# A gated MLP on one Trainium2 core: three steps of the gate change engines

## Chip, cores, metric

The kernel runs on one core of one Trainium2 chip, in one launch. The metric is the device time of an execution in microseconds (us); lower is better.

## What is computed

Three parts follow each other: an attention in which a query sees only the keys of its own cluster, a mixing by Fourier transforms with a plain MLP, and a gated MLP with a convolution of width 3 along the sequence. Batch 2, sequence 768, model width 512. The change touches the last part alone:

```python
def _moe2_ref(x, w_in, conv_w, w_out) -> np.ndarray:   # x (2, 768, 512), d_ff 1024
    h = np.maximum(x @ w_in, 0.0)
    ...
    for k in range(K):                                  # K = 3
        conv_out += conv_w[k][None, None, :] * hp[:, k:k + S, :]
    gate = 1.0 / (1.0 + np.exp(-conv_out))
    return (h * gate @ w_out).astype(np.float32)
```

`hp` is `h` with a zero row before and behind.

## The kernel before, in words

The engines are TensorE (PE; matmuls, with PEld for its weight loads), VectorE (DVE, `V` in the code), ScalarE (ACT, `A`), GpSimd (POOL, `G`) and SyncE (SP), which issues the DMAs here.

Products are made in near fp32 precision from pairs of numbers: a value is split into a high part, its cast to fp32r, and a low part, the value less the high one. `pass3` (lines 77 to 80) adds three matmuls for each product: high times high (L78), and the two mixed ones (L79, L80).

The gated MLP (from line 901 on) works in 16 blocks: two batches `b`, and in each eight blocks `f` of 128 hidden features. The features lie on the partitions, the 768 positions of the sequence in a row's elements. Each block has two halves.

- `mlp2_up(b, f)`, lines 797 to 815. `split_w` casts the block's weights to their high part on ScalarE (L778, `whb`) and makes the low part on POOL (L780, `wlb`). TensorE makes `u` in two halves of 384 positions, 12 matmuls each, in one of two PSUM banks by turns; ScalarE's relu (L806) empties each bank into `h2`. `h2` has a column of zero on either side (the memsets L801, L802). Then the gate: VectorE makes the convolution in three steps, a product (L808) and two products with a sum (L809, L810), in the tile `cv`; ScalarE makes the sigmoid in place (L811), POOL multiplies by `h2` (L812), VectorE casts to the high part `gH` (L814) and subtracts for the low part `gL` (L815).
- `down(1, b, f, side)`, lines 817 to 836. For each of six tiles of 128 positions three matmuls add to that tile's own PSUM bank `acc`. After the last block of a batch, VectorE and ScalarE by turns copy the six banks to `y`, one of three buffers (L833, L835), from where SyncE sends them out (L836).

The loop on lines 905 to 908 calls `mlp2_up` two blocks ahead of `down`. `cv`, `h2`, `gH` and `gL` have two buffers each, the split weights four. In the first six calls of `down`, `side` is `gate_in(1)` (lines 838 to 855): after the third tile TensorE transposes one tile of the second batch's input into one of the two banks of `u`, ScalarE casts it (L853), and VectorE subtracts for the low part (L854). The order on each engine is fixed when the program is built, by the scheduler of the tile framework; each engine works through its own queue in order, and an instruction that waits holds up all behind it.

Of the kernel before, what the change touches and what calls it, by code (L numbers as in the profile page):

```python
# [15 lines left out]
AF = mybir.ActivationFunctionType  # L16
ALU = mybir.AluOpType
# [3 lines left out]
B, H, S, D = 2, 8, 768, 64  # L21
# [21 lines left out]
def tile_net(ctx, tc, qk, v, cen, w12, w34, conv, dft, odd, out):  # L43
    nc = tc.nc
    V, A, G, T = nc.vector, nc.scalar, nc.gpsimd, nc.tensor

    def f32(ap):
        return ap.bitcast(F32)
# [186 lines left out]
    def norm(b, bank, lp):  # L235

        X = U[:, 6 * b:6 * b + 6, :]
        stats, ys, os = {}, {}, {}

        def stat(t):  # L240
            if b not in uns:
                uns[b] = up_[b].tile([128, 2, 4, S], F32R, tag="un", bufs=1, name=f"un{b}")
            st = lp.tile([128, 6], F32, tag="st", bufs=2, name=f"st{b}{t}")
            V.bn_stats(st, X[:, t])
            mv = lp.tile([128, 2], F32, tag="mv", bufs=3, name=f"mv{b}{t}")
            V.bn_aggr(mv, st)
            rs = lp.tile([128, 1], F32, tag="rs", bufs=3, name=f"rs{b}{t}")
            V.tensor_scalar(rs, mv[:, 1:2], 1e-6, None, ALU.add)
            stats[t] = (mv, rs)

        def root(t):
            rs = stats[t][1]
            G.tensor_tensor(rs, rs, half[:, 2:3], ALU.pow)

        def scale(t):
            mv, rs = stats[t]
            y = ys[t] = lp.tile([128, DM], F32, tag="y", bufs=1, name=f"y{b}{t}")
            V.tensor_scalar(y, X[:, t], mv[:, 0:1], rs, ALU.subtract, ALU.mult)

        def swap(t):  # L260
            o = os[t] = bank(f"unT{b}{t}").rearrange("p (c n) -> p c n", c=4)
            for c in range(4):
                T.transpose(o[:, c], ys[t][:, 128 * c:128 * c + 128], ident)
            A.copy(uns[b][:, 0, :, 128 * t:128 * t + 128], o)

        def low(t):
            tk = slice(128 * t, 128 * t + 128)
            V.tensor_sub(uns[b][:, 1, :, tk], os[t], f32(uns[b][:, 0, :, tk]))

        return stat, root, scale, swap, low  # L270
# [30 lines left out]
    def up_half(o, w, x, i):  # L301
        tk = slice(384 * i, 384 * i + 384)
        for c in range(4):
            sl = slice(128 * c, 128 * c + 128)
            pass3(o, w[0][:, sl], w[1][:, sl], x[:, 0, c, tk], x[:, 1, c, tk], c == 0, c == 3)
# [4 lines left out]
    with ExitStack() as actx:  # L310
# [7 lines left out]
        def slot(name):  # L318
            turn[0] = (turn[0] + 1) % 3
            return ps.tile([128, 2, 512], F32, tag=f"s{turn[0]}", bufs=1, name=name)  # L320
# [37 lines left out]
        t = slot("warm_up")  # L358
# [27 lines left out]
        for i in range(2):  # L386
            t = ap.tile([128, NT, 2, 130], F16, name=f"V16_{i}")
# [273 lines left out]
        stat, root, scale, swap, low = norm(0, lambda name: slot(name)[:, 0], dp)  # L661
# [111 lines left out]
    def up_bank(name):  # L773
        return bank("up", 2, name)

    def split_w(p, bufs, k, f, name, eng=G):
        wh = p.tile([128, 1024], F32R, tag="wh", bufs=bufs, name=f"wh{name}")
        A.copy(wh, w32[k, f])  # L778
        wl = p.tile([128, 1024], F32R, tag="wl", bufs=bufs, name=f"wl{name}")
        eng.tensor_sub(wl, w32[k, f], f32(wh))  # L780
        return wh[:, 0:512], wl[:, 0:512], wh[:, 512:1024], wl[:, 512:1024]
# [15 lines left out]
    def mlp2_up(b, f):  # L797
        gp = gps[0]
        w = ws[1, b, f] = split_w(gp, 4, "b", f, f"b{b}_{f}")
        h2 = gp.tile([128, S + 2], F32, tag="h2", bufs=2, name=f"h2{b}{f}")  # L800
        V.memset(h2[:, 0:1], 0.0)  # L801
        V.memset(h2[:, S + 1:S + 2], 0.0)  # L802
        for i in range(2):
            o = up_bank(f"u{b}{f}{i}")[:, 0:384]
            up_half(o, w, xs[b], i)
            A.activation(h2[:, 1 + 384 * i:385 + 384 * i], o, AF.Relu)  # L806
        t = gp.tile([128, S], F32, tag="cv", bufs=2, name=f"cv{b}{f}")
        V.tensor_scalar(t, h2[:, 0:S], cw[:, 3 * f:3 * f + 1], None, ALU.mult)  # L808
        V.scalar_tensor_tensor(t, h2[:, 1:S + 1], cw[:, 3 * f + 1:3 * f + 2], t, ALU.mult, ALU.add)  # L809
        V.scalar_tensor_tensor(t, h2[:, 2:S + 2], cw[:, 3 * f + 2:3 * f + 3], t, ALU.mult, ALU.add)  # L810
        A.activation(t, t, AF.Sigmoid)  # L811
        G.tensor_mul(t, t, h2[:, 1:S + 1])  # L812
        g = hs[1, b, f] = [gp.tile([128, S], F32R, tag=n, bufs=2, name=f"{n}{b}{f}") for n in ("gH", "gL")]
        V.tensor_copy(g[0], t)  # L814
        V.tensor_sub(g[1], t, f32(g[0]))  # L815

    def down(s, g, f, side, when=(2,)):
# [60 lines left out]
    cw = wp.tile([128, 24], F32, tag="cw", bufs=1, name="cw")  # L878
# [22 lines left out]
    gps.append(pool(ctx, "gp", side="right"))  # L901
    side = gate_in(1)
    mlp2_up(0, 0)
    mlp2_up(0, 1)
    for n in range(8 * B):
        if n + 2 < 8 * B:
            mlp2_up((n + 2) // 8, (n + 2) % 8)
        down(1, n // 8, n % 8, side)
# [72 lines left out]
```

## Time and profile before

| | |
|---|---|
| median of 3 runs | 752.48 us (lowest 751.13; one of the three took 2342.31) |
| the profiled execution | 750.55 us |
| its span (first to last instruction) | 748.8 us |
| TensorE busy | 698.7 us, 93% |
| VectorE busy | 536.4 us, 72% |
| ScalarE busy | 345.9 us, 46% |
| POOL busy | 271.2 us, 36% |
| granted clock of TensorE, mean | 0.979 |
| the gated MLP | from about 595 us to the end |

All times of the trace are counted from the start of the span. A row of the timeline gives the start, the duration, the engine, the line, the operation, its output and inputs, their shapes, how often it occurs in the row, and in square brackets how long the engine stood idle just before it and what ended that wait. Matmuls follow each other in a pipeline, so the duration of one is longer than the step from one to the next. The releaser is the event that came last, and need not be the one that had been missing longest.

### The profile page before, as it was taken

To read this page: it belongs to the slowest core of one execution; us is meant where nothing else is said; L and a number is where in the kernel's file an instruction comes from. 1 tells how busy PE (TensorE), PEld (TensorE's weight loads), DVE (VectorE), ACT (ScalarE), POOL (GpSimd) and SP (SyncE) were. 2 spreads that over 40 slices of the span, in tenths; PEclk is the share of its full clock that TensorE was granted. 3 is DMA by queue.
4 is the path that set the end of the run, shared out by engine and by line. 5 is a ranking of instruction groups with operands and counts; after the bars stand their busy time and mean duration, and the time that the engine had idled before them with its cause. 6 is when DMAs were issued, how large, how long until landed. Compare 5 with 4: busy or idle time off the path is not lost.

```text
span 748.8 us, 12517 instructions
## 1 busy us (share of the span) xinstructions
PE 698.7 (93%) x5090; PEld 623.2 (83%) x5090; DVE 536.4 (72%) x754; ACT 345.9 (46%) x492; POOL 271.2 (36%) x189
## 2 busy tenths in 40 slices
PE   8898999897998996989999999999999999999996
PEld 6787788786897885878988899999999788898984
DVE  7778989679977998999379937765111268777664
ACT  3576868586466685334234433433222233333321
POOL 8154644455244544131041003222232154443441
PEclk9999999999799999899999999999999999999999
DMA  7637678462533431214104321430000000002002
GB/s 219 173 78 209 184 196 251 107 196 59 157 71 79 92 116 59 98 71 169 57 0 169 116 109 57 168 113 1 1 0 1 1 0 1 1 1 84 1 1 84
DMA packets 19937, 66.47 MB, mean 89 GB/s; under 512 B 2868, under 2 KB 5928, under 8 KB 16808
## 3 DMA queue, kind: packets, MB, share of 16 engines
q1 hardware_dynamic: 19448, 61.93, 28.5%
q0 software_dynamic: 432, 3.75, 1.5%
q8 instruction: 40, 0.66, 0.3%
q14 instruction: 17, 0.14, 0.1%
HBM read 40.94 MB, written 5.77 MB: 62 GB/s over the span
## 4 chain that ended last, share of the span: by engine, by line
PE 48%; DVE 34%; ACT 5%; DMA 4%; POOL 4%; issue 3%; SPq 1%; POOLq 0%; DVEq 0%
PE up L78 5%; DVE m L533 5%; PE up L80 5%; PE up L79 5%; PE acc L80 5%; PE acc L78 5%; PE acc L79 5%; DVE gH L814 5%; DMA vraw<-v 3%; POOL cv L812 3%; PE av L590 3%; PE t L562 2%; DVE cv L809 2%; PE s L528 2%; DVE cv L810 2%
## 5 line engine op out<-in xcount | busy, mean ns | idle before, releaser
L578 POOL TENSOR_TENSOR p<-p,p 128x768 f16<-128x768 f32 x61 | 109.7, 1802 | 115.4 <-ACT p L573 81.7
L566 ACT ACTIVATE p<-t,cbias 128x768 f32<-128x768 f32 x96 | 86.2, 898 | 54.1 <-PE t L564 44.3
L533 DVE TENSOR_REDUCE m<-s 128x1 f32<-128x768 f32 x96 | 90.1, 943 | 13.1 <-PE s L530 6.7
L80 PE MATMUL up<-un,wla 128*128 128x384 f32 x248 | 83.9, 339 | 1.6 <-DVE wla L780 1.6
L78 PE MATMUL up<-un,wha 128*128 128x384 f32 x248 | 84.1, 339 | 0.7 <-DVE YsL L178 0.5
L780 POOL TENSOR_TENSOR wla<-wa,wha 128x1024 fp32r<-128x1024 f32 x16 | 38.5, 2404 | 126.6 <-ACT wha L778 126.6
L79 PE MATMUL up<-un,wha 128*128 128x384 f32 x248 | 83.9, 338 | 0.0
L795 DVE SCALAR_TENSOR_TENSOR hL<-up,hH 128x384 fp32r<-128x384 f32 x62 | 34.2, 552 | 65.6 <-ACT hH L794 65.4
L590 PEld LDWEIGHTS <-p 128*128 128x128 f16 x1728 | 61.1, 100 | 21.6 <-issue 15.4
L590 PE MATMUL av<-V,p 128*128 128x65 f16 x1728 | 73.2, 197 | 5.4 <-POOL p L578 3.6
L573 ACT CAST p<-p 128x768 f16<-128x768 f32 x91 | 75.5, 830 | 1.5
L78 PE MATMUL acc<-wha,hH 128*128 128x512 f32 x186 | 73.7, 396 | 0.0
L80 PE MATMUL acc<-wha,hL 128*128 128x512 f32 x186 | 72.7, 391 | 0.0
L79 PE MATMUL acc<-wla,hH 128*128 128x512 f32 x186 | 72.5, 390 | 0.0
L562 PE MATMUL t<-X 128*128 128x384 f32 x192 | 55.6, 371 | 16.8 <-DVE m L533 14.2
L794 ACT ACTIVATE hH<-up 128x384 fp32r<-128x384 f32 x62 | 30.4, 490 | 75.0 <-PE up L80 74.9
L528 PE MATMUL s<-X 128*128 128x384 f32 x192 | 57.0, 379 | 5.9 <-DVE m L533 4.7
L814 DVE CAST gH<-cv 128x768 fp32r<-128x768 f32 x16 | 35.3, 2209 | 31.3 <-POOL cv L812 31.3
L778 ACT CAST wha<-wa 128x1024 fp32r<-128x1024 f32 x31 | 32.5, 1048 | 52.2 <-PE acc L80 46.3
L812 POOL TENSOR_TENSOR cv<-cv,h 128x768 f32<-128x768 f32 x16 | 25.4, 1590 | 78.1 <-ACT cv L811 78.1
L562 PEld LDWEIGHTS t<-X 128*128 128x128 f32 x192 | 31.9, 193 | 25.1 <-DVE m L533 15.8
L530 PE MATMUL s<-Y 96*128 96x384 f32 x192 | 50.6, 345 | 1.2 <-DMA Y<-G 1.2
(311 smaller groups left out, 1652.0 us busy)
## 6 DMA issues: line engine op xcount, KB each, us to landing
rawa<-w SPq DMA_DIRECT2D x14, 1024.0 KB
rawb<-w SPq DMA_DIRECT2D x8, 1024.0 KB
raw<-qk SPq DMA_DIRECT2D x7, 768.0 KB
X<-G SPq DMA_DIRECT2D x14, 384.0 KB
Y<-G SPq DMA_DIRECT2D x14, 384.0 KB
DC<-dft POOLq DMA_DIRECT2D x2, 1671.0 KB, 7.1
vraw<-v SPq DMA_DIRECT2D x8, 384.0 KB
out<-y SPq DMA_DIRECT2D x12, 256.0 KB
```

Of the source, the lines that this page charges most:

```text
L78: T.matmul(o, sH, mH, start=start, stop=False)
L79: T.matmul(o, sH, mL, start=False, stop=False)
L80: T.matmul(o, sL, mH, start=False, stop=stop)
L528: T.matmul(t[:, c, 0:384], X[:, 0, sl], X[:, 1, 384 * c:384 * c + 384], start=True, stop=False)
L530: T.matmul(t[:, c, 0:384], Y[0:96, 0, sl], Y[0:96, 1, 384 * c:384 * c + 384], start=False, stop=True)
L533: V.tensor_reduce(m6s[h][:, i:i + 1], t[:, :, 0:384], AX.XY, ALU.max, negate=True)
L562: T.matmul(t[:, c, 0:384], X[:, 1, sl], X[:, 0, 384 * c:384 * c + 384], start=True, stop=False)
L566: A.activation(p.rearrange("p (c n) -> p c n", c=2), t[:, :, 0:384], AF.Exp, bias=cbias, scale=0.125)
L573: A.copy(p16[:, 0], p32s[n])
L578: eng.tensor_sub(p16[:, 1], p, p16[:, 0])
L590: T.matmul(o, p16[:, k, 128 * j:128 * j + 128], v16[:, i, h % 2, 65 * part:65 * part + 65], start=(i + j + k + part == 0), stop=(i == 5), ...
L814: V.tensor_copy(g[0], t)
```

## The change

Three lines of `mlp2_up` change engines, and no value that they compute. The convolution's first product goes from VectorE to ScalarE, as an activation Copy with the weight as its scale. The product of the gate and `h2` goes from POOL to VectorE. The cast to `gH` goes from VectorE to ScalarE.

```diff
@@ def mlp2_up(b, f)
         t = gp.tile([128, S], F32, tag="cv", bufs=2, name=f"cv{b}{f}")
-        V.tensor_scalar(t, h2[:, 0:S], cw[:, 3 * f:3 * f + 1], None, ALU.mult)
+        A.activation(t, h2[:, 0:S], AF.Copy, scale=cw[:, 3 * f:3 * f + 1])
         V.scalar_tensor_tensor(t, h2[:, 1:S + 1], cw[:, 3 * f + 1:3 * f + 2], t, ALU.mult, ALU.add)
         V.scalar_tensor_tensor(t, h2[:, 2:S + 2], cw[:, 3 * f + 2:3 * f + 3], t, ALU.mult, ALU.add)
         A.activation(t, t, AF.Sigmoid)
-        G.tensor_mul(t, t, h2[:, 1:S + 1])
+        V.tensor_mul(t, t, h2[:, 1:S + 1])
         g = hs[1, b, f] = [gp.tile([128, S], F32R, tag=n, bufs=2, name=f"{n}{b}{f}") for n in ("gH", "gL")]
-        V.tensor_copy(g[0], t)
+        A.copy(g[0], t)
         V.tensor_sub(g[1], t, f32(g[0]))
```

The scheduler orders the queues anew. On VectorE, in a block of the second batch (`cv_7473` is this block's convolution, `h_7442` its `h2`, `gH_7479` and `gL_7480` its parts; `h_7568` is the `h2` of a later block):

```order
-L808 TENSOR_SCALAR cv_7473<-h_7442,cw 128x768
 L809 SCALAR_TENSOR_TENSOR cv_7473<-h_7442,cw,cv_7473 128x768
 L810 SCALAR_TENSOR_TENSOR cv_7473<-h_7442,cw,cv_7473 128x768
-L814 CAST gH_7479<-cv_7473 128x768
+L812 TENSOR_TENSOR cv_7473<-cv_7473,h_7442 128x768
 L801 MEMSET h_7568 128x1
 L802 MEMSET h_7568 128x1
 L815 TENSOR_TENSOR gL_7480<-cv_7473,gH_7479 128x768
```

The product stands where the cast stood, and the first product of the convolution is gone from the queue.

On ScalarE, in the same block (`whb_5_7564` is the high part of the weights two blocks on; the two relus that follow belong to the next block, `h_7505`):

```order
 L806 ACTIVATE h_7442<-u_7445 128x384
 L806 ACTIVATE h_7442<-u_7459 128x384
+L808 ACTIVATE cv_7473<-h_7442,cw 128x768
 L811 ACTIVATE cv_7473<-cv_7473 128x768
 L778 CAST whb_5_7564<-wb_6216 128x1024
+L814 CAST gH_7479<-cv_7473 128x768
 L806 ACTIVATE h_7505<-u_7508 128x384
 L806 ACTIVATE h_7505<-u_7522 128x384
+L808 ACTIVATE cv_7536<-h_7505,cw 128x768
```

The cast to `gH` stands between the weight cast and the next block's relus.

On ScalarE in the opening (`h_6710`, `h_6755` and `h_6800` are the `h2` of blocks 0, 1 and 2, `gH_6747` is the high part of block 0):

```order
 L806 ACTIVATE h_6710<-u_6713 128x384
 L806 ACTIVATE h_6710<-u_6727 128x384
+L808 ACTIVATE cv_6741<-h_6710,cw 128x768
 L806 ACTIVATE h_6755<-u_6758 128x384
 L811 ACT_TABLE_LOAD
 L811 ACTIVATE cv_6741<-cv_6741 128x768
 L806 ACTIVATE h_6755<-u_6772 128x384
+L808 ACTIVATE cv_6786<-h_6755,cw 128x768
+L814 CAST gH_6747<-cv_6741 128x768
 L806 ACTIVATE h_6800<-u_6803 128x384
 L806 ACTIVATE h_6800<-u_6817 128x384
+L808 ACTIVATE cv_6831<-h_6800,cw 128x768
```

Block 1's first product and block 0's cast now stand in front of block 2's relus. On TensorE the one difference is in the first `acc`: its first L80 stands behind the L78 and L79 of the second tile too.

## Rows read from the trace of the kernel before

**Rows 1.** The page, section 4: the chain that ended last, by engine.
```profile
PE 48%; DVE 34%; ACT 5%; DMA 4%; POOL 4%; issue 3%; SPq 1%; POOLq 0%; DVEq 0%
PE up L78 5%; DVE m L533 5%; PE up L80 5%; PE up L79 5%; PE acc L80 5%; PE acc L78 5%; PE acc L79 5%; DVE gH L814 5%; DMA vraw<-v 3%; POOL cv L812 3%; PE av L590 3%; PE t L562 2%; DVE cv L809 2%; PE s L528 2%; DVE cv L810 2%
```
**Rows 2.** Busy time by stage: window, its length, each engine, PEclk, DMA share, GB/s.
```profile
690.00:735.00 45.00, 45.00 (x223) 40.27 (x222) 30.84 (x35) 12.20 (x20) 17.27 (x9) 1.00 0.01 5
```
**Rows 3.** Timeline of VectorE: one block, and the last block's L809.
```profile
698.56 1.02 DVE L809 SCALAR_TENSOR_TENSOR cv<-h,cw,cv 128x768 f32<-128x768 f32 x1
...
703.23 2.77 DVE L814 CAST gH<-cv 128x768 fp32r<-128x768 f32 x1 [2.60 <-POOL cv L812]
...
706.10 0.96 DVE L815 TENSOR_TENSOR gL<-cv,gH 128x768 fp32r<-128x768 f32 x1
...
707.63 1.02 DVE L809 SCALAR_TENSOR_TENSOR cv<-h,cw,cv 128x768 f32<-128x768 f32 x1
...
732.63 1.02 DVE L809 SCALAR_TENSOR_TENSOR cv<-h,cw,cv 128x768 f32<-128x768 f32 x1
```
**Rows 4.** Timelines of ScalarE and of POOL in the same block.
```profile
700.66 0.85 ACT L811 ACTIVATE cv<-cv 128x768 f32<-128x768 f32 x1 [5.96 <-DVE cv L810]
701.41 1.03 ACT L778 CAST whb<-wb 128x1024 fp32r<-128x1024 f32 x1
702.35 0.87 ACT L806 ACTIVATE h<-u 128x384 f32<-128x384 f32 x2
...
701.65 1.55 POOL L812 TENSOR_TENSOR cv<-cv,h 128x768 f32<-128x768 f32 x1 [5.14 <-ACT cv L811]
703.16 2.42 POOL L780 TENSOR_TENSOR wlb<-wb,whb 128x1024 fp32r<-128x1024 f32 x1
```
**Rows 5.** Timeline of TensorE: first matmuls of `u`, of `acc`, and of the next `u`.
```profile
698.21 0.34 PE L78 MATMUL u<-x,whb 128*128 128x384 f32 x1
...
702.45 0.40 PE L78 MATMUL acc<-whb,gH 128*128 128x512 f32 x1
...
706.65 0.34 PE L78 MATMUL u<-x,whb 128*128 128x384 f32 x1
```
**Rows 6.** Timeline of TensorE from 606 us on: the rows with a wait.
```profile
608.39 0.44 PE L78 MATMUL u<-x,whb 128*128 128x384 f32 x1 [0.41 <-ACT h L806]
...
612.38 0.50 PE L80 MATMUL acc<-whb,gL 128*128 128x512 f32 x1 [1.06 <-DVE gL L815]
619.51 0.44 PE L78 MATMUL u<-x,whb 128*128 128x384 f32 x1 [0.59 <-DVE h L802]
...
647.40 0.42 PE L78 MATMUL u<-x,whb 128*128 128x384 f32 x1 [1.01 <-DVE x L854]
...
688.98 0.50 PE L78 MATMUL acc<-whb,gH 128*128 128x512 f32 x1 [1.11 <-DVE y L833]
...
737.91 0.50 PE L78 MATMUL acc<-whb,gH 128*128 128x512 f32 x1 [1.58 <-DVE gH L814]
738.98 0.50 PE L80 MATMUL acc<-whb,gL 128*128 128x512 f32 x1 [0.33 <-DVE gL L815]
```
**Rows 7.** Timelines of POOL and VectorE: the opening, and a `gH` late in the stage.
```profile
595.41 9.80 POOL L780 TENSOR_TENSOR wlb<-wb,whb 128x1024 fp32r<-128x1024 f32 x4 [17.01 <-PE acc L79]
...
602.97 3.06 DVE L809 SCALAR_TENSOR_TENSOR cv<-h,cw,cv 128x768 f32<-128x768 f32 x1
...
730.44 0.56 DVE L814 CAST gH<-cv 128x768 fp32r<-128x768 f32 x1 [2.60 <-POOL cv L812]
```
**Rows 8.** Busy time by stage, as rows 2: one microsecond of the last `acc`.
```profile
740.00:741.00 1.00, 1.00 (x4) 0.72 (x4) 0.20 (x1) 0.10 (x1) 0.00 (x0) 0.50 0.07 20
```
**Rows 9.** Timeline of the end: first output copy, last matmul, last output copy.
```profile
739.52 0.58 ACT L835 COPY y<-acc 128x512 f32<-128x512 f32 x1 [3.94 <-PE acc L80]
...
744.13 0.39 PE L80 MATMUL acc<-whb,gL 128*128 128x512 f32 x1
...
744.82 0.69 DVE L833 COPY y<-acc 128x512 f32<-128x512 f32 x1 [0.92 <-DMA out<-y]
```
**Rows 10.** The chain that ended last, in order of time: start, length, what.
```profile
742.69 2.01 DMA out<-y
```

## Prediction

> **What bounds the kernel now.** I read the chain of waits first. In the whole span it is TensorE for about half and VectorE for a third, and among its costliest steps stand VectorE's cast L814 (gH) [rows 1]. All lines of the change lie in the second MLP, so I went to that stretch. The table by stage shows a puzzle: from 690 to 735 us TensorE is busy in all of the time at full clock [rows 2], and still VectorE could matter. To see why, I laid one feature block f (16 of them: two batches of eight) beside itself on each engine.
>
> VectorE's block takes from the start of one L809 to the next 9.07 us (698.56 to 707.63) [rows 3]. Every step of it hands on: L809 and L810 2.10 together, then the sigmoid on ScalarE (0.99 until POOL starts), POOL's product L812 (1.58 until gH starts), gH 2.87 until gL starts, then gL and the next block's L808, 1.53 [rows 3, 4]. The sum is 9.07, so this is a closed ring with no slack. TensorE's block is 24 `u` matmuls in 4.24 us and 18 `acc` matmuls in 4.20, together 8.44 [rows 5]. The ring is thus 0.63 us a block slower than TensorE. TensorE doesn't show it at once, since `up` runs two blocks ahead of `down`; it eats up the lead, and waits at the end.
>
> So I listed every place where TensorE waits behind a line of the change [rows 6]. The bracket is the idle time; as matmuls overlap (0.34 us long at a step of 0.177, 0.39 at 0.233), the loss from start to start is the bracket plus 0.16. That gives 0.57 (608.39, ScalarE's relu held up behind a sigmoid), 1.22 (612.38, gL), 0.75 (619.51, the memset row is only the last event; the relu stood behind the sigmoid and the weight cast), 1.17 (647.40, an x transpose's bank not yet read by VectorE), 1.27 (688.98, an accumulator of the first batch not yet copied by VectorE, which was at gH and gL), 1.74 and 0.49 (737.91 and 738.98, gH and gL of the last block). Together 7.2 us. Behind the last two the granted clock is 0.50, that is 1.2 GHz, in the row of 740 to 741 [rows 8]; TensorE had been idle for 1.58 and 0.33 us just before it fell [rows 6]. From 738.98 to the last matmul at 744.13 there are 15 steps, which at 0.233 are 3.5 us and took 5.15: another 1.65 [rows 6, 9]. All that the change can win is about 8.9 us, 1.2% of the time.
>
> **The change part by part.** Per block VectorE loses L808 and gH and gets the product; POOL loses the product and keeps only the weight split L780; ScalarE gets L808 and gH.
>
> *The product on VectorE.* The nearest row is gL, which also reads two fp32 tiles: 0.96 us; the dearest is L809 at 1.02 [rows 3]. I take 0.96, against POOL's 1.55 [rows 4].
>
> *L808 and gH on ScalarE.* Not seen there before. The nearest row is the sigmoid on the same 128x768, 0.85; above lies the cast of 128x1024 at 1.03, below half of the pair of relus on 128x384, 0.43 [rows 4]. I take 0.85 each. gH thus gets dearer than its free price on VectorE, 0.56 (730.44) [rows 7], but cheaper than the 2.77 that it costs beside L780.
>
> *Who holds whom.* gH took 2.77 where POOL's L780 (2.42) had started 0.07 us earlier, and 0.56 where POOL had nothing left to do [rows 3, 4, 7]. L809 at 602.97 took 3.06 while four L780 filled POOL from 595.41 on, and 1.02 later [rows 3, 7]. So VectorE's work on two SBUF tiles and POOL's shut each other out. The Trainium skill says so in "SBUF — State Buffer", section "Who interferes with whom": a VectorE instruction with two SBUF inputs and a GpSimd one that reads SBUF can't run together, and the one that comes second waits for the whole of the first. The trace agrees (3.06 against 1.02). By that rule the new product is as exposed as gH was, and gL too.
>
> Which of them meets L780? L780 needs the weight cast L778, which ScalarE issues after the sigmoid and which starts 0.75 after it; with its 1.03 and 0.14 to the start on POOL (as from sigmoid to product, [rows 4]) L780 begins 1.9 us after the sigmoid's start. The product can start 0.95 after it and is through at 1.9, so it comes first. gL, after gH on ScalarE, would start at 2.85 and comes second. gH ended 0.42 after L780 did (706.00 against 705.58), so I expect gL at 5.2, a record of some 2.3 us in place of 0.96. This costs nothing: it lies beside matmuls, as the next sum shows. It would cost if gL were wanted within 9 us of `u`.
>
> *The new chain against TensorE.* Let T be the end of a block's `u` (the start of the next `acc`, 702.45 in the block shown). The relu pair ends at T+0.77 [rows 4, 5]. Then L808 to 1.66, L809 and L810 to 3.77, sigmoid 3.80 to 4.65, product 4.75 to 5.71, gH to 6.60, gL to 7.6, or to 9.0 if held. `acc` of this block starts only after two more blocks' worth of matmuls, at T+16.9. So in the steady blocks nothing waits. In the last block no `u` lies between: `acc` 13 and 14 take 8.40, then gH is wanted at T+8.4 and gL 0.47 later. Nothing is left on POOL by then, so they are there 1.8 and 1.3 us early. The last waits (1.74 and 0.49) go, and the clock has no pause behind which to fall (1.65).
>
> *New orders on ScalarE.* gH of block f waits for the product and stands in front of the relus of f+1. As a ring: relus 0.87, L808 0.89, L809 and L810 2.10, sigmoid 0.95, product 1.01, gH 0.89, in all 6.7 us a block. This is under TensorE's 8.44, so the bank of `u` is read in time. The x copies (L853, L854) and the output copies lie beside L809 and the sigmoid on whichever of the two engines is free then.
>
> *The opening.* L809 of block 0 still can't run before POOL's fourth L780 is through (602.97 to 606.03 now [rows 7]). L808 no longer delays that L780, so I take 0.3 off, and the 0.57 at 608.39 shrinks to 0.27. By the steps above its product is then through at 608.7; ScalarE does L808 of block 1 first and gH to 609.6, VectorE L809 of block 1 first and gL to 610.8. TensorE starts `acc` at 610.3 and wants gL at 611.2, since its first L80 now stands behind four matmuls where it stood behind two. The 1.22 goes. Relu 3 is no longer behind sigmoid 2 at its late hour: 0.75 goes. 1.17 and 1.27 go because the copies that TensorE waits for there no longer stand on VectorE behind a held gH.
>
> *The end.* From the last `acc`'s start to the last output copy it takes 6.91 us now (737.91 to 744.82) [rows 6, 9]. At full clock a tile takes 0.70. The copy of tile 5 needs tile 2's buffer (three of them), so its landing: 1.87 us to tile 2's last matmul, 0.54 to the copy (from the last matmul of a tile at 738.98 to 739.52), 0.58 the copy, 2.01 the transfer, 0.15 the issue: 5.15 [rows 6, 9, 10]. The transfer now hides part of the clock's 1.65. Gain 1.76.
>
> **Sum.** 0.3 + 1.22 + 0.75 + 1.17 + 1.27 + 1.74 + 1.76 = 8.2 us. The profiled execution took 750.55 (span 748.8 and 1.75 around it), the median of the runs shown is 752.48 and the lowest 751.13. From 751.5 in their midst the forecast is 743.3. Bounds: 8.9 less what the end hides is the most that waits can give back; the least, with ScalarE's two at 1.03 and all waits of the opening kept, is about 4.8.
>
> **Rivals.**
> *A, the opening keeps its waits* (0.20). In the first blocks ScalarE gets L808 and gH in front of relus that TensorE waits for, with a margin of only 0.4 us at gL; and the x copy at 647 comes to stand behind the product. For it: two of the early waits already run through ScalarE. Against: the product leaves POOL and its late start. The gains up to 647 (3.4) stay away: 8.2 less 3.4 is 4.8, time 746.7.
> *B, slower: the ring through ScalarE decides* (0.05). Its place is gH in front of the next relus, its price whatever lengthens the ring beyond 6.7. The second half of block 3's `u` begins now at 619.51, so this `u` ends at 621.6; less the 2.3 won by then it is 619.4, and L809 follows 1.7 later at 621.1. L809 of block 15 stands at 732.63 [rows 3]. With eleven rings and a last one of 6.7 (no weights are left to split) it comes later than that from a ring of 9.5 on. If the product were held for one L780 it would end 2.9 later, 0.42 behind POOL; the ring is then 9.6, and L809 of block 15 0.8 late, a tie. At 9.9 it is 736.7, some 4 us late, time 755.5. Against it: the product's lead of 0.95 us on L780. By the lock rule of the Trainium skill, above, the product is held if POOL gets there first.
> *C, more than the waits* (0.07): with the product gone from POOL the matmuls step faster, say by 1% of 16 blocks of 8.44, 135 us: another 1.4, and with the rest of the opening's 0.57 some 1.7, time 741.6. No row speaks for it.
> *D, the clock falls at the end all the same* (0.08): 1.5 of the 1.76 stays, time 744.8.
>
> **How the numbers follow.** The forecast has 0.60. It, C and D lie between 741 and 745; A lies at 746.7, B around and beyond 751. With the spread of the runs shown (1.4 us) on either side, and up to the foot of B, I take 740.5 to 750.5. A measurement of this kernel can tell about 2%, 15 us, from no change. No case with a place in the trace wins 15 us, and B needs a ring of 10.9 to lose them: faster 0.02, within 0.96, slower 0.02.
>
> **What would show it.** gL and no longer gH held by L780 (some 2.3 us beside 0.96), the product at 0.96, L808 and gH on ScalarE at 0.85, the L809 step at TensorE's 8.44, no wait of TensorE on gH or gL in the last block, and the clock at 1.00 behind 730. Wrong would be: a product of over 2 us, relus that start late behind gH with TensorE idle on `u`, or a last block that waits again.

## The result and the profile after

The changed kernel takes 742.39 us (median of 4 runs, 740.63 to 745.13) against 751.81 for the kernel before (4 runs beside it). The ratio of the fast runs is 0.9891, with a 95% interval of 0.9848 to 0.9934; one run before took 2342.31 us, which lifts that median and stands outside the ratio. The change makes the kernel about 1% faster, inside the 2% that counts as no change. The forecast was 743.3. The profiled execution took 740.75 with a span of 739.0; before it was 750.55 and 748.8.

The start of the second MLP shifts by up to 6 us from trace to trace, behind work whose lines the change doesn't touch. So I compare what I call the stage: from the first `u` matmul to the end of the span. Before it lasts 153.46 us (595.34 to 748.8), after 144.82 (594.18 to 739.0). The gain is 8.64, the forecast's sum 8.2. The other 1.16 of the 9.8 us between the spans lies ahead of the stage.

The chain that ended last, by engine and by line (the page of the kernel after, section 4):

```profile
PE 66%; DVE 21%; DMA 5%; ACT 3%; issue 3%; POOL 1%; SPq 1%; DVEq 0%; POOLq 0%; ACTq 0%
PE acc L78 8%; PE acc L79 8%; PE acc L80 8%; PE up L78 5%; PE up L80 5%; PE up L79 5%; DVE m L533 5%; DMA vraw<-v 4%; PE av L590 3%; PE u L80 3%; PE u L78 3%; PE u L79 3%; PE s L528 3%; PE t L562 3%; PE t L564 2%
```

TensorE has risen from 48% to 66% and VectorE has fallen from 34% to 21% [rows 1]. gH, the product and the two sums, four of the costliest steps of before, are no longer listed; the three lines of `u` are. From 600 to 730 us the chain now runs through matmuls for 95% of the time.

The table by stage, kernel after (window, its length, busy time of TensorE, weight loads, VectorE, ScalarE, POOL, then the granted clock, DMA share, GB/s):

```profile
690.00:728.00 38.00, 38.00 (x188) 33.87 (x187) 22.66 (x25) 18.87 (x25) 7.32 (x3) 1.00 0.00 1
730.00:731.00 1.00, 1.00 (x6) 0.80 (x5) 0.00 (x0) 0.24 (x1) 0.00 (x0) 1.00 0.00 0
```

In the first row VectorE is busy for 60% of the time where it was 69% (30.84 of 45 us), ScalarE for 50% where it was 27% [rows 2]. TensorE is busy throughout in both; this row alone could not tell which kernel is the faster. The second row lies in the last `acc`, where the clock before was 0.50 [rows 8]: now it is 1.00.

VectorE's timeline, kernel after: one steady block, then the last gL and the last output copy:

```profile
697.83 1.02 DVE L809 SCALAR_TENSOR_TENSOR cv<-h,cw,cv 128x768 f32<-128x768 f32 x1 [1.22 <-ACT cv L808]
698.88 1.02 DVE L810 SCALAR_TENSOR_TENSOR cv<-h,cw,cv 128x768 f32<-128x768 f32 x1
700.82 0.96 DVE L812 TENSOR_TENSOR cv<-cv,h 128x768 f32<-128x768 f32 x1 [0.91 <-ACT cv L811]
...
702.68 2.38 DVE L815 TENSOR_TENSOR gL<-cv,gH 128x768 fp32r<-128x768 f32 x1 [0.77 <-ACT gH L814]
706.27 1.02 DVE L809 SCALAR_TENSOR_TENSOR cv<-h,cw,cv 128x768 f32<-128x768 f32 x1 [1.22 <-ACT cv L808]
...
728.05 0.96 DVE L815 TENSOR_TENSOR gL<-cv,gH 128x768 fp32r<-128x768 f32 x1 [0.96 <-ACT gH L814]
...
735.01 0.69 DVE L833 COPY y<-acc 128x512 f32<-128x512 f32 x1 [0.82 <-ACT y L835]
```

One L809 to the next takes 8.44 us (697.83 to 706.27), where the ring took 9.07 [rows 3]. VectorE now stands idle ahead of the first sum, the product and gL: it follows TensorE and no longer sets the pace. gL is the one that is held, 2.38 against 0.96 at the end.

ScalarE and POOL in the same block, kernel after:

```profile
696.86 0.94 ACT L808 ACTIVATE cv<-h,cw 128x768 f32<-128x768 f32 x1
699.94 0.85 ACT L811 ACTIVATE cv<-cv 128x768 f32<-128x768 f32 x1 [2.14 <-DVE cv L810]
700.69 1.03 ACT L778 CAST whb<-wb 128x1024 fp32r<-128x1024 f32 x1
701.81 0.84 ACT L814 CAST gH<-cv 128x768 fp32r<-128x768 f32 x1
...
701.80 2.45 POOL L780 TENSOR_TENSOR wlb<-wb,whb 128x1024 fp32r<-128x1024 f32 x1 [6.00 <-ACT whb L778]
```

The product (700.82 to 701.78) is through 0.02 us before L780 starts, as the forecast had it (both at 1.9 after the sigmoid's start); gL comes 0.88 behind L780 and ends 0.81 after it (705.06 against 704.25).

TensorE, kernel after: a block's `u` and `acc`, the place where it waited at the opening, and the last `acc`:

```profile
606.49 0.34 PE L80 MATMUL u<-x,wlb 128*128 128x384 f32 x1
606.96 0.44 PE L78 MATMUL u<-x,whb 128*128 128x384 f32 x1
...
700.34 0.34 PE L78 MATMUL u<-x,whb 128*128 128x384 f32 x1
...
704.57 0.40 PE L78 MATMUL acc<-whb,gH 128*128 128x512 f32 x1
...
708.78 0.34 PE L78 MATMUL u<-x,whb 128*128 128x384 f32 x1
...
733.82 0.40 PE L80 MATMUL acc<-whb,gL 128*128 128x512 f32 x1
```

The block's 8.44 is unchanged (700.34 to 708.78) [rows 5]. Of the seven waits of [rows 6] one is left, at 606.96: a step of 0.47 where 0.177 is free, a loss of 0.29. And one stands that the change doesn't touch, on the low part of block 0's weights (at 596.66). The table of waits lists no other for TensorE and its weight loads in the stage (who waits for whom, us in total, times, longest):

```profile
PE u L80 <- POOL wlb L780: 1.6, 1, 1.6
PEld u L78 <- ACT h L806: 0.5, 1, 0.5
```

### The profile page after: what moved, and what is told of

Same layout as the page of the kernel before. It is cut to its first block, busy times and chain, and to the rows that moved or that the text cites. A ratio compares the mean times of both kernels' runs of the same rounds, so it can differ in the third digit from the quotient of the medians.

```text
span 739.0 us, 12486 instructions
## 1 busy us (share of the span) xinstructions
PE 692.7 (94%) x5090; PEld 619.8 (84%) x5090; DVE 521.6 (71%) x738; ACT 375.5 (51%) x524; POOL 246.3 (33%) x173
## 4 chain that ended last, share of the span: by engine, by line
PE 66%; DVE 21%; DMA 5%; ACT 3%; issue 3%; POOL 1%; SPq 1%; DVEq 0%; POOLq 0%; ACTq 0%
PE acc L78 8%; PE acc L79 8%; PE acc L80 8%; PE up L78 5%; PE up L80 5%; PE up L79 5%; DVE m L533 5%; DMA vraw<-v 4%; PE av L590 3%; PE u L80 3%; PE u L78 3%; PE u L79 3%; PE s L528 3%; PE t L562 3%; PE t L564 2%
## 5 line engine op out<-in xcount | busy, mean ns | idle before, releaser
L80 PE MATMUL up<-un,wla 128*128 128x384 f32 x248 | 83.9, 339 | 1.6 <-DVE wla L780 1.6
L78 PE MATMUL up<-un,wha 128*128 128x384 f32 x248 | 84.1, 339 | 0.7 <-DVE YsL L178 0.5
L79 PE MATMUL up<-un,wha 128*128 128x384 f32 x248 | 83.8, 338 | 0.0
L780 POOL TENSOR_TENSOR wla<-wa,wha 128x1024 fp32r<-128x1024 f32 x16 | 38.5, 2406 | 126.5 <-ACT wha L778 126.5
L78 PE MATMUL acc<-wha,hH 128*128 128x512 f32 x186 | 73.6, 396 | 0.0
L80 PE MATMUL acc<-wha,hL 128*128 128x512 f32 x186 | 72.6, 391 | 0.0
L79 PE MATMUL acc<-wla,hH 128*128 128x512 f32 x186 | 72.5, 390 | 0.0
L780 POOL TENSOR_TENSOR wlb<-wb,whb 128x1024 fp32r<-128x1024 f32 x16 | 39.0, 2445 | 96.4 <-ACT whb L778 79.4
L778 ACT CAST wha<-wa 128x1024 fp32r<-128x1024 f32 x31 | 32.5, 1049 | 52.1 <-PE acc L80 46.2
L564 PE MATMUL t<-Y 98*128 98x384 f32 x192 | 50.3, 343 | 0.7 <-DMA Y<-mr 0.6
```

The costliest lines, as they stand in the source:

```text
L78: T.matmul(o, sH, mH, start=start, stop=False)
L79: T.matmul(o, sH, mL, start=False, stop=False)
L80: T.matmul(o, sL, mH, start=False, stop=stop)
L564: T.matmul(t[:, c, 0:384], Y[0:98, 1, sl], Y[0:98, 0, 384 * c:384 * c + 384], start=False, stop=True)
```

## Experiments

Times in one group are ratios to runs of the kernel before on the same chip. The expectations in microseconds go by 751.5 for the kernel before; it took 749.41 beside `p0_all` to `p3_cast`, and 750.13 and 749.39 beside the later ones, so I compare gains. Stage lengths are from one profiled execution each. The changed kernel run a second time (`p0_all`) gave 144.78 us where the first gave 144.82, so I read differences of a few tenths.

| kernel | ratio, 95% interval | stage, us |
|---|---|---|
| before | 1 | 153.46 |
| after | 0.9891, 0.9848 to 0.9934 | 144.82 |
| p0_all | 0.9874, 0.9835 to 0.9913 | 144.78 |
| p1_conv | 0.9892, 0.9851 to 0.9932 | 145.78 |
| p2_prod | 0.9894, 0.9847 to 0.9941 | 145.96 |
| p3_cast | 0.9903, 0.9865 to 0.9941 | 146.28 |
| b0_only | 0.9926, 0.9894 to 0.9957 | 147.41 |
| b1_only | 0.9949, 0.9917 to 0.9981 | 148.65 |
| dup1 | 0.9932, 0.9892 to 0.9971 | 148.77 |
| dup3 | 1.0295, 1.0247 to 1.0344 | 172.19 |
| dup3_nolock | 0.9978, 0.9945 to 1.0011 | 152.09 |
| dupc2 | 0.9898, 0.9833 to 0.9964 | 145.03 |
| no_sums | 0.9869, 0.9816 to 0.9923 | 144.54 |
| better | 0.9857, 0.9810 to 0.9905 | 141.74 |

### One part at a time

The theory was that any part that takes the ring under TensorE's 8.44 us brings most of the gain. Its rival was that gH has to leave VectorE, since it is gH that L780 holds. From the kernel before, one line each:

```diff
p1_conv
-        V.tensor_scalar(t, h2[:, 0:S], cw[:, 3 * f:3 * f + 1], None, ALU.mult)
+        A.activation(t, h2[:, 0:S], AF.Copy, scale=cw[:, 3 * f:3 * f + 1])
p2_prod
-        G.tensor_mul(t, t, h2[:, 1:S + 1])
+        V.tensor_mul(t, t, h2[:, 1:S + 1])
p3_cast
-        V.tensor_copy(g[0], t)
+        A.copy(g[0], t)
```

> Only the convolution's first product goes to ScalarE; the gate's product stays on POOL and the cast to gH on VectorE. Theory (the ring on VectorE against TensorE's pace): the ring loses L808's 0.65 and comes to 8.42 us a block, TensorE's own pace, so nearly all waits go: 743 to 745 us, gH still about 2.77 us long. Rival (what counts is that gH leaves VectorE, where POOL holds it): gH is still held, so the waits at the end stay: 749 to 751 us.

> Only the gate's product goes from POOL to VectorE. Theory (ring against pace): the product starts 0.95 us after the sigmoid does and is through at 1.9, when POOL's weight split starts too; gH then runs first or is held to POOL's end, and the ring is 8.0 to 8.5 us a block: 743 to 746 us, with a little left of the waits of the opening, since L808 stays on VectorE. Rival (gH must leave VectorE): 749 to 751 us.

> Only the cast to gH goes to ScalarE; the product stays on POOL. Theory (ring against pace): gL is now held to the end of POOL's weight split, about 2.5 us, and the ring is about 8.55 us a block: 744 to 746 us. Rival (gH must leave VectorE): this part alone brings all, 742 to 743 us, and more than either of the other two by 5 us or more.

> The change as it is, beside its three parts on one chip: 741 to 744 us by either theory. If the three parts added up, each alone would bring about a third of its 9 us; by the ring they don't add, and each alone brings most of it.

The three parts alone shorten the stage by 7.68, 7.50 and 7.18 us; all three together by 8.64 (8.68 in `p0_all`). Each brings 83 to 89% of the whole, and their sum would be 22.4. Times say the same: the four intervals overlap almost entirely. VectorE's timeline with L808 alone moved (`p1_conv`):

```profile
707.53 1.01 DVE L809 SCALAR_TENSOR_TENSOR cv<-h,cw,cv 128x768 f32<-128x768 f32 x1
...
712.20 2.77 DVE L814 CAST gH<-cv 128x768 fp32r<-128x768 f32 x1 [2.60 <-POOL cv L812]
...
715.95 1.01 DVE L809 SCALAR_TENSOR_TENSOR cv<-h,cw,cv 128x768 f32<-128x768 f32 x1
```

gH is held for its full 2.77 as before [rows 3], and still the step is 8.42 and the last block waits for nothing. So the rival falls: the hold didn't cost anything by itself, it cost as one link of a ring that was 0.63 us too long. With the cast alone moved (`p3_cast`) the hold goes over to gL, as the durations of that line show (shortest, median, longest in ns, then first and last start):

```profile
L815 DVE TENSOR_TENSOR gL<-cv,gH x16: 953/2286/2301, 609.8 to 729.8; 128x768 fp32r<-128x768 f32 x16
```

What the single parts leave lies in the first batch: `p2_prod` and `p3_cast` keep 0.41 of idle time behind the relu at 607, `p3_cast` also 0.74 behind gL at 610.82, and `p1_conv` and `p2_prod` keep 0.37 and 0.40 behind an x transpose's bank (642.85 and 643.82).

### One batch at a time

The forecast's waits lie in two groups: up to 647 us in the first batch, the last two in the second. So the three edits were made for one batch of blocks alone.

```diff
b0_only (b1_only has b == 1); the other two lines likewise
+        if b == 0:
+            A.activation(t, h2[:, 0:S], AF.Copy, scale=cw[:, 3 * f:3 * f + 1])
+        else:
+            V.tensor_scalar(t, h2[:, 0:S], cw[:, 3 * f:3 * f + 1], None, ALU.mult)
```

> The change in the eight blocks of the first batch alone. Theory: the waits of the opening (3.7 us at 608, 612, 619 and 647 in the trace of before) and the one at the first batch's accumulators (1.27) go; in the second batch the ring of 9.07 us against 8.44 eats the lead, and TensorE waits 1.5 to 2.5 us for gH and gL of the last block and the clock falls to 1.2 GHz behind it: 5 us faster than before, about 746.5. Rival (only the average speed of the ring counts, not where): half of the change's gain, with no wait at the end.

> The change in the eight blocks of the second batch alone. Theory: the waits of the opening stay (3.7 us), those at the first batch's accumulators and of the last block go, and the clock doesn't fall at the end: 4 to 5 us faster than before, about 746.8. Together with the first batch alone that is the whole gain. If the fall of the clock at the end has another cause than the wait before it, it is still there.

`b1_only` came out as worked: 4.81 us, with all the opening's waits kept and none at the end. `b0_only` gained 6.05 where 5 was expected. Its opening's waits are gone and the last block's are there, which the rival didn't allow for. On TensorE's timeline (L823 is the cast to gH, L824 gL, as they were before):

```profile
732.12 0.50 PE L78 MATMUL acc<-whb,gH 128*128 128x512 f32 x1 [1.60 <-DVE gH L823]
...
733.18 0.50 PE L80 MATMUL acc<-whb,gL 128*128 128x512 f32 x1 [0.34 <-DVE gL L824]
```

These are the 1.58 and 0.33 of [rows 6] over again. But the clock did not fall behind them (`b0_only`, by stage, columns as above):

```profile
733.00:734.00 1.00, 0.82 (x4) 0.68 (x5) 0.13 (x1) 0.28 (x1) 0.00 (x0) 1.00 0.00 0
734.00:735.00 1.00, 1.00 (x6) 0.82 (x5) 0.57 (x1) 0.31 (x1) 0.00 (x0) 1.00 0.00 0
735.00:736.00 1.00, 1.00 (x6) 0.82 (x5) 0.12 (x1) 0.59 (x1) 0.00 (x0) 1.00 0.73 270
```

So the part of the expectation on the clock missed. A pause of 1.6 us ahead of the last `acc` was followed by 1.2 GHz in the kernel before and by 2.4 GHz here. That the pause alone makes the clock fall is refuted; what else it took stays open. Every fall between the stage's first and last matmul, in all the traces kept, comes right behind a pause of TensorE. The clock is also part of why the two halves add up to 10.86 us where the whole gives 8.64: both keep the clock at 1.00, and the wait of 1.27 at 688.98 is gone in both.

### Loading ScalarE

Rival B said that the ring through ScalarE decides once it is long enough. To find its edge I let ScalarE do L808 twice (`dup1`) and four times (`dup3`), and the cast to gH twice (`dupc2`).

```diff
dup1 (dup3 has three such lines), from the kernel after
         A.activation(t, h2[:, 0:S], AF.Copy, scale=cw[:, 3 * f:3 * f + 1])
+        A.activation(t, h2[:, 0:S], AF.Copy, scale=cw[:, 3 * f:3 * f + 1])
dupc2
         A.copy(g[0], t)
+        A.copy(g[0], t)
```

> The changed kernel with L808 issued twice in a row in every block (the same values are written again): 0.94 us more in ScalarE's ring, 7.6 us a block. Theory: under TensorE's 8.44, so within 1 us of the changed kernel. Rival (ScalarE is the bound after the change, or near it): 16 x 0.9, some 10 us or more slower than the changed kernel.

> The changed kernel with L808 issued four times in a row in every block (the same values are written again): 2.8 us more in ScalarE's ring, 9.5 us a block. Theory: over TensorE's 8.44 by 1.0 (0.6 where a transpose lies in the block), less 1.3 us of lead in the last block: 9 to 12 us slower than the changed kernel, 751 to 755, with TensorE waiting for gH of the last block, or for a bank of u behind a late relu. Rival (ScalarE's queue has still room, as it is busy for half of the time): within 2 us of the changed kernel.

> The changed kernel with the cast to gH issued twice in a row (the same values are written again); here the weight cast stays behind the sigmoid, so POOL's split still meets gL and no sum. The ring through ScalarE is 7.5 us. Theory: under TensorE's 8.44, so no more than 0.5 us on the stage from the first u matmul to the end (144.8 us in the trace of the changed kernel). Rival (the earlier run with one more L808 was 4 us slower because of ScalarE's load): 3 to 5 us more here too.

The second cast cost 0.2 us in 16 blocks, as expected: 0.84 more on ScalarE and behind it nothing late. The copies of L808 missed by far, +3.95 and +27.4 us. `dup1` shows why. Its ScalarE, POOL, VectorE and TensorE timelines, where a line number from L809 on is one more than in the kernel after (L811 is the second sum, L812 the sigmoid, L815 the cast to gH, L855 VectorE's read of an x transpose):

```profile
623.10 1.05 ACT L778 CAST whb<-wb 128x1024 fp32r<-128x1024 f32 x1
627.50 0.84 ACT L812 ACTIVATE cv<-cv 128x768 f32<-128x768 f32 x1 [3.35 <-DVE cv L811]
...
624.23 2.43 POOL L780 TENSOR_TENSOR wlb<-wb,whb 128x1024 fp32r<-128x1024 f32 x1 [6.87 <-ACT whb L778]
...
653.40 2.39 POOL L780 TENSOR_TENSOR wlb<-wb,whb 128x1024 fp32r<-128x1024 f32 x1 [4.61 <-ACT whb L778]
...
624.30 3.17 DVE L811 SCALAR_TENSOR_TENSOR cv<-h,cw,cv 128x768 f32<-128x768 f32 x1
...
654.09 2.51 DVE L813 TENSOR_TENSOR cv<-cv,h 128x768 f32<-128x768 f32 x1 [1.48 <-ACT cv L812]
...
608.72 0.50 PE L78 MATMUL acc<-whb,gH 128*128 128x512 f32 x1 [1.03 <-ACT gH L815]
...
645.20 0.42 PE L78 MATMUL u<-x,whb 128*128 128x384 f32 x1 [1.75 <-DVE x L855]
```

The scheduler put the weight cast L778 ahead of the sigmoid. L780 then starts 0.07 us before VectorE's second sum, which takes 3.17 us in place of 1.02; in a later block (654.09) it is the product that is held, 2.51. Sum and product are links of the ring, gL is not. In the three blocks with a held sum the step is 9.8 to 10.2 us, and TensorE waits 0.60 (634.25) and 1.75 (645.20) for a bank that VectorE reads late. The third wait of the stage, 1.03 at 608.72, has nothing to do with the hold: there gH stands behind the doubled L808 on ScalarE, and no lead covers it. These three are nearly all of the 3.95. In seven later blocks the product is held too and takes 2.2 us, and the step is 8.41 to 8.88 without a wait of TensorE: a held link costs nothing while the ring stays within TensorE's own step.

In `dup3` nine of the sixteen second sums (L813 there) are held, the step from one first sum to the next is 10.0 to 11.1 us in most of these blocks, and TensorE waits at thirteen places besides block 0's weights: for gH (2.63 at 751.82 and 2.43 at 760.46 among them), for banks that VectorE and ScalarE read late, and for weights.

Two causes were left for `dup3`: ScalarE's 2.8 us more a block, or the hold. `dup3_nolock` keeps all the work on ScalarE and takes the weight subtraction off POOL from block 4 on, by having VectorE do it (1.22 us of its own time).

```diff
-        w = ws[1, b, f] = split_w(gp, 4, "b", f, f"b{b}_{f}")
+        w = ws[1, b, f] = split_w(gp, 4, "b", f, f"b{b}_{f}", G if (b, f) < (0, 4) else V)
```

> L808 issued four times as in the run before, but from the fifth block on the weights' low part (L780) is made by VectorE (1.22 us each) and POOL is idle. In the trace of the run before, L780 had moved beside VectorE's second sum, which took 3.17 us in place of 1.02, and the ring was 10.0 to 11.1 us; less that hold of 2.15 it would be 7.85 to 8.9. Theory (two SBUF operands against POOL, one holds the other inside the ring): about TensorE's 8.44 again, 743 to 749 us. Rival (ScalarE's queue is too long with three more activations of 0.94): still 765 us or more.

It is 20.1 us shorter in the stage than `dup3` (172.19 to 152.09), though VectorE has more to do. The second sum's durations in `dup3`, then in `dup3_nolock`:

```profile
L813 DVE SCALAR_TENSOR_TENSOR cv<-h,cw,cv x16: 1003/3145/3183, 610.2 to 756.6; 128x768 f32<-128x768 f32 x16
```

```profile
L813 DVE SCALAR_TENSOR_TENSOR cv<-h,cw,cv x16: 1008/1019/1020, 606.1 to 732.4; 128x768 f32<-128x768 f32 x16
```

So 20 of the 27 us go with the hold inside the ring, with two of the three falls of the clock in `dup3` among them (0.66 over 615 to 620 and over 700 to 705, 0.71 over 750 to 755; `dup3_nolock` has only the first, 0.73 over 610 to 615). The other 7.3 come with ScalarE's load; VectorE's 1.22 a block is in them too, and no run takes the two apart. Most of the 7.3 lies at the two ends, where no lead covers a longer chain (`dup3_nolock`, TensorE's timeline):

```profile
612.04 0.60 PE L78 MATMUL acc<-whb,gH 128*128 128x512 f32 x1 [3.27 <-ACT gH L817]
...
736.30 0.50 PE L78 MATMUL acc<-whb,gH 128*128 128x512 f32 x1 [1.58 <-ACT gH L817]
```

The Trainium skill states in "SBUF — State Buffer", section "Who interferes with whom", that a VectorE instruction with two inputs in SBUF and a GpSimd instruction that reads SBUF take turns, the later one waiting for the whole of the earlier. The trace agrees: L811 of `dup1` ends at 627.47, 0.81 us after L780's 626.66, and the product at 654.09 the same 0.81 after its L780 (656.60 against 655.79), as if nearly all of their work began only then.

### Is anything of the gate still on the path?

If the rest of VectorE's chain still cost time, leaving out the convolution's two sums, 2.10 us a block, would show it.

```diff
no_sums, from the kernel after
-        V.scalar_tensor_tensor(t, h2[:, 1:S + 1], cw[:, 3 * f + 1:3 * f + 2], t, ALU.mult, ALU.add)
-        V.scalar_tensor_tensor(t, h2[:, 2:S + 2], cw[:, 3 * f + 2:3 * f + 3], t, ALU.mult, ALU.add)
```

> The changed kernel without the convolution's two sums (L809, L810 are left out, so the gate sees the first product alone): 2.1 us less in the ring, VectorE down to two long operations a block. Theory: TensorE is the bound in every block already, so the stage from the first u matmul to the end stays at 144.8 us, less at most 0.3 in the opening: the time of the changed kernel, 740.5 to 744. Rival (the gate's chain still costs in places that the waits don't show): 2 us or more faster.

It gains 0.3 us, which is the 0.29 left at 606.96; no such step is left in its trace. The change has used up what this chain has to give.

### A version that goes on from there

What the stage still has is the 1.62 us on block 0's weights and the last copy's wait for a buffer. So block 0's subtraction was cut in halves, and the output copies got six buffers.

```diff
better, from the kernel after
-        eng.tensor_sub(wl, w32[k, f], f32(wh))
+        for lo, hi in ((0, 512), (512, 1024)) if name == "b0_0" else ((0, 1024),):
+            eng.tensor_sub(wl[:, lo:hi], w32[k, f][:, lo:hi], f32(wh)[:, lo:hi])
...
-                    y = gps[0].tile([128, 512], F32, tag="y", bufs=3, name=f"y{g}{t}")
+                    y = gps[0].tile([128, 512], F32, tag="y", bufs=6, name=f"y{g}{t}")
```

> The changed kernel with what its trace still shows: the first block's low part is made in two halves on POOL, so that u waits 1.2 us less for the first of them, and y has six buffers in place of three, so that the last copy needs no landing (5.15 us from the last acc's start to the last copy, then about 4.5). Theory: 1.1 and 0.65, the stage 143.1 us in place of 144.8, the ratio to the kernel before about 0.986. Rival (the opening's wait returns behind the other splits): 0.6 or less.

The stage is 141.74, 3.1 us shorter than after and 1.4 better than expected. From the last matmul's start to the last output copy's it takes 0.43 us (734.43 to 734.86) where after has 1.19 (733.82 to 735.01). No wait of TensorE on another engine is left in the stage, but the halves did not do that. POOL's timeline in the kernel after, and then in `better`:

```profile
594.25 7.12 POOL L780 TENSOR_TENSOR wlb<-wb,whb 128x1024 fp32r<-128x1024 f32 x3 [17.00 <-PE acc L79]
```

```profile
590.61 4.91 POOL L781 TENSOR_TENSOR wlb<-wb,whb 128x512 fp32r<-128x512 f32 x3 [10.48 <-ACT whb L778]
```

After, the first split waited for the last `acc` of the first MLP, whose memory its tile takes over; in `better` it is released by its own cast, ahead of the first `u`. I take it that six buffers moved the tiles in memory; neither edit was run alone. And a shorter stage is not yet a faster kernel: here the stage began late, at 597.06, the span is 738.8 against 739.0, and the interval (0.9810 to 0.9905) overlaps that of the change. That it beats the change is not shown.

## Why the prediction was right

**The ring against TensorE.** Right. Every part that brings the ring to TensorE's 8.44 or below brings most of the gain alone, and the step in the second batch becomes 8.40 to 8.47 in nearly every block of each of them. `no_sums` shows that a still shorter ring brings nothing. One thing the forecast passed over: six blocks of the first batch also hold a transpose, and there TensorE's own step is 8.86 to 8.87, before and after. The ring of 9.07 was 0.63 too long only in the others, and 0.2 in these six.

**The waits listed.** Right in that 1.22, 0.75, 1.17, 1.27, 1.74 and 0.49 are gone from the trace, and the 0.57 is 0.29 (0.27 was forecast). Rival A, that the opening keeps them, fell. Two of the reasons were wrong. The 0.75 at 619.51 was laid to a relu behind the sigmoid and the weight cast. VectorE, then ScalarE, kernel before:

```profile
618.77 0.68 DVE L854 TENSOR_TENSOR x<-xT,x 128x512 fp32r<-128x512 f32 x1
...
619.71 0.48 ACT L806 ACTIVATE h<-u 128x384 f32<-128x384 f32 x1
```

That relu starts 0.20 us after the matmul that it was said to hold up. What ends just before the matmul (at 619.45) is VectorE's read of the first transpose, whose bank this half of `u` takes next, so the wait is of the same kind as the 1.17 at 647.40. And the 1.17 and 1.27 were to go because VectorE's copies no longer stand behind a held gH. In `p1_conv` gH is held as before, and still the 1.27 is gone and 0.37 of idle time is left of the 1.17: what counted was how late the ring ran, and not the hold.

**The end.** The 5.15 us that the forecast built up from tile 2's landing is what the trace has, by two misses that cancel (TensorE's and VectorE's timelines and the chain that ended last, kernel after):

```profile
729.86 0.39 PE L78 MATMUL acc<-whb,gH 128*128 128x512 f32 x1
...
732.77 2.13 DMA out<-y
...
735.01 0.69 DVE L833 COPY y<-acc 128x512 f32<-128x512 f32 x1 [0.82 <-ACT y L835]
```

The chain that ended last goes through this landing, at 734.90; ScalarE's copy of tile 4, which the row names, ended at the same time. The transfer took 2.13 where 2.01 was taken, and tile 2's copy began 2.29 after the last `acc` where 2.41 was taken. The step on the clock came out (1.00 behind 730, so D fell), but a pause isn't enough to make the clock fall: in `b0_only` it stayed up behind the same pause. Only one execution of the kernel before was traced, so that the 1.65 is lost in every one is not shown.

**Prices.** The product 0.96 as taken; gH on ScalarE 0.83 (0.85 taken); L808 on ScalarE 0.94, inside its bounds of 0.43 to 1.03 but 0.09 over the sigmoid's price. It lies beside matmuls, and moved nothing.

**Who holds whom.** Right: gL in place of gH, with a median of 2.38 us (2.3 was forecast), at no cost. The forecast's ground was too narrow for gH, though. Its rule is for two inputs in SBUF, and gH is a cast with one, `cv`. That gH is held on VectorE all the same only the trace showed (2.77 against 0.56). On ScalarE it begins 0.01 after L780 (701.81 and 701.80) and takes 0.84, about as long as with POOL idle (0.83 in the last block).

**What the sum left out.** 8.2 was forecast and 8.64 measured. The rest lies at the waits, which the forecast priced 0.1 to 0.2 too low each. It took the loss as the bracket and 0.16, but the step behind the waiting matmul is longer too. Behind 612.38 [rows 6] the next starts at 612.72, a step of 0.34 where 0.233 is free:

```profile
612.72 0.39 PE L78 MATMUL acc<-whb,gH 128*128 128x512 f32 x1
```

Compared stretch by stretch, from one first matmul of `u` or `acc` to the next, the four waits from 612 to 689 cost 1.41, 0.87, 1.25 and 1.36 us; the forecast had 1.22, 0.75, 1.17 and 1.27. That is 0.48 more, which covers the 0.45 that was missing. Stretches without a wait or a transpose are the same before and after, 4.23 to 4.24 for `u` and 4.20 to 4.21 for `acc`, so Rival C, faster steps, fell too.

**Rival B.** It didn't happen, since the product began 0.98 us ahead of L780 (0.95 was forecast). That its mechanism is real `dup1` and `dup3` show: with the second sum held, the step became 9.8 to 11.1 us in most such blocks, and `dup3` slower than the kernel before (1.0295). What the forecast left out is that L778's place, which decides who meets L780, is the scheduler's choice and can turn with one more instruction on ScalarE. The lead of 0.95 holds for the order it was worked out for, and says nothing of another.

## What to carry to other kernels

Where one engine is busy throughout and the time still hangs on another, compare their steps for one block: work taken from the longer ring pays until it is as short as the other's step, and then not at all, so that here the first cheap edit brought most of it. Ask of every instruction that can be held by another engine whether it is a link of that ring; 1.4 us of hold a block cost nothing on gL, and 2.1 us on nine sums went with 20 us. And look at what a scheduler does with the new order before an instruction is called free.

## What was unexpected

- The clock. Idle times of 1.58 and 0.33 us ahead of the last `acc` were followed by 1.2 GHz in the kernel before, 1.60 and 0.34 at the same place in `b0_only` by 2.4 GHz throughout. In `dup3` the granted clock is 0.71 over 750 to 755, around the wait of 2.63 at 751.82, and 1.00 over 760 to 765, behind the wait of 2.43 at 760.46. The length of a pause alone doesn't tell whether the clock falls.
- One more activation of 0.94 us a block on ScalarE, with slack there in the steady blocks, cost 3.95 us. The larger part is not on ScalarE: through the order of the weight cast it made VectorE's second sum three times as long (3.17 against 1.02) in three blocks.
- An activation that only copies and scales 128x768 takes 0.94 us on ScalarE, more than a sigmoid (0.85) or a cast (0.84) of that size in the same block. It is the only one of the three whose scale is read from a tile; no run here shows whether that is why.
